# Dividing two more pairs of softmax rows ahead of their transposition, and starting the second batch's attention five steps earlier

## The chip, the cores and the metric

The kernel runs on one core of a Trainium2 chip. Its time is the device time of one execution in microseconds (us). Three executions of the kernel before took 2164.79 us (median), 2163.91 and 2167.59 us. Below, PE is the engine of the matrix multiplications (PEld its loading of the stationary operand), DVE the vector engine, ACT the scalar engine, POOL the general-purpose engine, and SP the engine that issues the DMA transfers.

## The reference: attention, a Fourier mix, and a two-layer network

```python
q_n, k_n = rmsnorm(q, g_q), rmsnorm(k, g_k)          # (8, 12, 448, 64)
scores = q_n @ k_n.T / 8
attn = exp(scores - max); attn = attn / (sum(attn) + 1e-9)
x = (attn @ v)  -> (8, 448, 768)                     # 8 batches, 12 heads side by side
X = fft(fft(x, axis=1), axis=2);  u = x + real(X)
un = (u - mean) / sqrt(var + 1e-6)
out = u + relu(un @ w_ch1) @ w_ch2                   # 768 -> 3072 -> 768
```

Everything is float32.

## The kernel before

**Batches and pairs.** A batch is one of 8 inputs of 448 tokens. Its 12 heads are handled as 6 pairs. In names such as `P0_4_2`, the numbers are batch, pair and row group: the 448 query rows of a pair are cut into 4 groups (c) of 112 rows.

**Attention of a pair** has three parts. `transpose_pair` loads q and k (`raw`), squares them on ACT, sums (`ss`), takes the power -1/2 on POOL, multiplies (`qkn`) and turns the two on PE (`qk`, copied by ACT to `QT` and `KD`). `softmax_pair` makes the scores `S` on PE, one bank per head, the row minimum `mn` on DVE, the exponential `P` with its row sum `sm` on ACT, and the reciprocal of `sm` on DVE. `value_pair` turns `P` (tiles `pt`, and a last piece `rem`), has ACT copy the turned tiles to `T` and `R`, and multiplies them with `v` into `av`; ACT copies that to `xT`.

**Two ways to divide the rows.** In batch 0 the rows stay undivided: DVE writes a diagonal matrix `dg` of the reciprocals, and the turning is a real matrix product of the piece with `dg`. In the other batches `P` is multiplied by the reciprocal first (head 0 on ACT and head 1 on DVE in batch 1) and the turning is PE's transposition against the identity `ident`.

**After attention.** `fold` (DVE: `eo`, `sd`, `tot`) adds and subtracts mirrored tokens and halves of the channels; `spectral` does the two Fourier steps as products (`y`, then `ab`), adds x back (`x`, `smdf`, `u`) and makes the centred rows `un`. `ffn_input` turns `un` into `unT`, and `ffn` runs the two layers, `h` (24 groups of 18 matmuls) and `o` (36 groups of 12), each product in three passes over high and low parts.

**What sets the order of work.** The attention and the spectral part are Python generators which give up control after each small step. The last part of the kernel first runs batch 0's generator alone: `for n, _ in enumerate(aux(0))`. It has 132 steps, n = 0 to 131: pair p = 5 of the attention takes n = 91 to 109, its values 110 to 120, a fold 121, the spectral part 122 to 131. At each step it may convert a part of the weights (`convert_some`; the conversions, `magw`, `dblw` and `w`, go through ACT, DVE and POOL in turn and are stored by DMA), and from n = `AHEAD_FROM` on it also takes one step of batch 1's generator, `second`. What `second` has not done by then is merged with batch 0's network by `merge`, in proportion to the costs that each step names. Within what is then written, a scheduler orders the instructions of each engine and places the waits. Each engine runs its own list strictly in order.

**Pair 0 of batch 1 has two callers.** In pair p = 5 of batch 0, `attention` calls `transpose_pair` for the next pair, which is pair 0 of batch 1. Batch 1's own generator begins with the same call. A test lets the second caller pass if the first has finished:

```python
        if b >= nb or (b, p) in ready:
            return
        load_pair(b, p)
        load_pair(*next_pair(b, p))
```

The first caller enters the pair into `ready` after its last step, when the loop that follows n = 109 resumes. `load_pair` loads nothing that still stands in `loaded`, but `norm_pair` takes the pair out of `loaded` when it begins.

**Banks.** A bank is one of eight accumulators of PE. `S` has two banks in rotation (also used by `y0_0_0`, `y0_1_0` and by `ab`), `PT` two (`pt`, `rem`, `y0_0_1`, `y0_1_1`), `ffn` two, `q` and `av` one each. PE cannot write a bank again before ACT or DVE has read it.

The functions that the diff touches, with the line numbers of the profile:

Of the kernel before, what the change touches and what calls it, by code (L numbers as in the profile page):

```python
# [43 lines left out]
DFT_STEP = 40  # L44
PLAIN_PAIRS = range(2 * NPAIR)
PLAIN_SCORES = range(2, 2 * NPAIR)
PACE = 3
LAG = 3
AHEAD_FROM = 112
AHEAD_STEPS = 1  # L50

MIN_HIGH = float(np.uint32(0x38000000).view(np.float32))
# [38 lines left out]
def spectral_block(ctx, tc, q, k, v, g_q, g_k, w1, w2, d1, d2, out, nb=B):  # L91
# [204 lines left out]
    def plain(b, p):  # L296


        return b * NPAIR + p in PLAIN_PAIRS

    def plain_s(b, p):
        return b * NPAIR + p in PLAIN_SCORES

# [56 lines left out]

    def softmax_pair(b, p, Pc):
        QT, KD, _ = ready[b, p]
        if b == 0:
            diags[b, p] = slot("h", f"dg{b}_{p}")[:C, : 8 * C].rearrange(
                "t (c h q) -> t c h q", c=NC, h=2
            )
        for c in range(NC):
            P = slot("P", f"P{b}_{p}_{c}")[:C, : 2 * S]
            Ph = [P[:, :S], P[:, S:]]
            mn = sb.tile([C, 2], F32, tag="mn", name=f"mn{b}_{p}_{c}", bufs=4)  # L370
            sm = sb.tile([C, 2], F32, tag="sm", name=f"sm{b}_{p}_{c}", bufs=4)
            cs = slice(c * C, (c + 1) * C)
            tag = "ffn" if b == 0 and c % 2 else "S"
            banks = [bank(tag, f"S{b}_{p}_{c}_{h}")[:C, :S] for h in range(2)]

            for h, s_ in enumerate(banks):
                hs = (lo, hi)[h]
                if plain_s(b, p):
                    nc.tensor.matmul(s_, QT[hs, cs], KD[hs], start=True, stop=True)  # L379
                    continue  # L380
                for step, K in enumerate((KD, KL)):
                    nc.tensor.matmul(  # L382
                        s_, QT[:, h, cs], K[:, h], start=step == 0, stop=step == 1
                    )
            for h, s_ in enumerate(banks):
                V.tensor_reduce(mn[:, h : h + 1], s_, axis=AX.X, op=ALU.min)
                A.activation(
                    Ph[h],
                    s_,
                    AF.Exp,  # L390
                    bias=mn[:, h : h + 1],
                    scale=-1.0,
                    accum_out=sm[:, h : h + 1],
                )
            A.activation(sm, sm, AF.Identity, bias=tiny[:C])
            V.reciprocal(sm, sm)
            if b == 0:
                V.tensor_tensor(
                    out=diags[b, p][:, c],
                    in0=ident[:C, None, :C].broadcast_to([C, 2, C]),  # L400
                    in1=sm[:, :, None].broadcast_to([C, 2, C]),
                    op=ALU.mult,
                )
                Pc.append(P)
                yield 760
                continue
            for h in range(2):
                if b < EARLY and h == 0:
                    A.activation(Ph[h], Ph[h], AF.Copy, scale=sm[:, h : h + 1])
                    continue  # L410
                V.tensor_scalar(
                    out=Ph[h], in0=Ph[h], scalar1=sm[:, h : h + 1], scalar2=None,
                    op0=ALU.mult,
                )
            Pc.append(P)
            yield 760

    def value_halves(b, p, Pc, xT, R):
# [3 lines left out]
        for j in range(3):  # L422
            T = []
            for h in range(2):
                pt = bank("PT", f"pt{b}_{p}_{h}_{j}")
                for c in range(NC):
                    piece = Pc[c][:, 512 * h + j * 128 : 512 * h + (j + 1) * 128]
                    if b == 0:
                        nc.tensor.matmul(  # L429
                            pt[:, c * C : (c + 1) * C], piece, diags[b, p][:, c, h],  # L430
                            start=True, stop=True,
                        )
                        continue
                    nc.tensor.transpose(
                        pt[:, c * C : (c + 1) * C], piece, ident[:C, :C]
                    )
                t = slot("PT", f"T{b}_{p}_{h}_{j}")[:, :S]
                copied = A.copy(t, pt[:, :S])
                T.append(t)
                yield 400  # L440
            for h, a in enumerate((lo, hi)):
                mm = nc.tensor.matmul(  # L442
                    av[a, :S], v_[:, j, h], T[h], start=j == 0, stop=False
                )
                if h == 0:
                    order(
                        mm, copied,
                        mybir.DependencyClass.Sync, mybir.DependencyReason.SCHED_ONLY,
                    )
            yield 800  # L450
# [8 lines left out]
    def value_pair(b, p, Pc, xT):  # L459
        vhl = ready[b, p][2]  # L460
        rem = bank("PT", f"rem{b}_{p}")
        for c in range(NC):
            if b == 0:
                for h, a in enumerate((lo, hi)):
                    nc.tensor.matmul(
                        rem[a, c * C : (c + 1) * C],
# [581 lines left out]
    for n, _ in enumerate(aux(0)):  # L1048
        if n == DFT_STEP:
            load_dft()  # L1050
        if n:
            convert_some(CONVERT_EARLY)
        if n >= AHEAD_FROM:
            for _ in range(AHEAD_STEPS):
                next(second, None)
    starting[0] = False
# [38 lines left out]
```

## Time and profile before

| | |
|---|---|
| median of three runs | 2164.79 us |
| the profiled execution | 2168.16 us, span 2166.3 us |
| mean granted clock of PE | 0.979 |
| PE busy | 2110.4 us (97% of the span) |
| DVE, ACT, POOL busy | 1523.5, 1122.6, 376.7 us |
| first matmul of the network of batch 0 (`h0_0`) | 188.87 us |

The profiled execution took 3.4 us more than the median of the runs. Rows of the timeline give the start and the length of each piece of work; in the chain of waits a piece is counted only as long as nothing else is ahead of it. A matmul of the program in plain float32 appears in the profile as two instructions, a transposition and a matmul of rounded halves as one. The granted clock says at what share of its full speed PE was allowed to run.

### The profile page before, as it was taken

To read this page: it belongs to the slowest core of one execution; us is meant where nothing else is said; L and a number is where in the kernel's file an instruction comes from. 1 tells how busy PE (TensorE), PEld (TensorE's weight loads), DVE (VectorE), ACT (ScalarE), POOL (GpSimd) and SP (SyncE) were. 2 spreads that over 40 slices of the span, in tenths; PEclk is the share of its full clock that TensorE was granted. 3 is DMA by queue.
4 is the path that set the end of the run, shared out by engine and by line. 5 is a ranking of instruction groups with operands and counts; after the bars stand their busy time and mean duration, and the time that the engine had idled before them with its cause. 6 is when DMAs were issued, how large, how long until landed. Compare 5 with 4: busy or idle time off the path is not lost.

```text
span 2166.3 us, 31520 instructions
## 1 busy us (share of the span) xinstructions
PE 2110.4 (97%) x11408; PEld 1845.1 (85%) x11408; DVE 1523.5 (70%) x2809; ACT 1122.6 (52%) x2462; POOL 376.7 (17%) x223
## 2 busy tenths in 40 slices
PE   7999999899999999999999999999999999999998
PEld 4555666789999999999999999999999999998998
DVE  6887778986885778758786678857787578743122
ACT  7877867465652566436652566526663466422100
POOL 4654555640110011001000001100110011000000
PEclk7988999999999999999999999999999999999999
DMA  6554867777556855667555765658555674459664
GB/s 198 183 161 143 258 237 214 250 261 221 160 166 185 252 164 167 193 189 220 173 168 176 236 185 173 192 171 234 179 176 177 206 213 147 152 172 280 196 214 151
DMA packets 294494, 422.12 MB, mean 195 GB/s; under 512 B 182994, under 2 KB 221315, under 8 KB 294340
## 3 DMA queue, kind: packets, MB, share of 16 engines
q1 hardware_dynamic: 293572, 419.43, 62.6%
q8 instruction: 91, 1.49, 0.3%
q10 hardware_dynamic: 768, 0.69, 0.1%
q14 instruction: 63, 0.52, 0.1%
HBM read 360.27 MB, written 65.28 MB: 196 GB/s over the span
## 4 chain that ended last, share of the span: by engine, by line
PE 86%; DVE 5%; ACT 2%; DMA 2%; issue 2%; POOL 1%; SPq 0%; POOLq 0%; DVEq 0%; ACTq 0%
PE h L981 30%; PE o L1002 30%; PE S L382 5%; PE av L502 4%; PE pt L490 4%; PE y L603 2%; DMA w<-w 2%; PE S L379 1%; PE qk L338 1%; PE pt L429 1%; PE av L442 1%; PE un L864 1%; PE x L635 1%; DVE magw L755 1%; PE oT L919 1%
## 5 line engine op out<-in xcount | busy, mean ns | idle before, releaser
L1002 PE MATMUL o<-hs,w 128*128 128x448 f32 x3420 | 776.7, 371 | 10.0 <-DMA w<-w 4.2
L981 PE MATMUL h<-unT,w 128*128 128x448 f32 x3402 | 767.6, 370 | 3.9 <-DMA w<-w 1.6
L1002 PEld LDWEIGHTS o<-hs,w 128*128 128x128 f32 x3420 | 634.2, 189 | 70.5 <-issue 12.2
L981 PEld LDWEIGHTS h<-unT,w 128*128 128x128 f32 x3402 | 628.8, 188 | 58.3 <-issue 4.8
L114 ACT ACTIVATE P<-S,mn 112x448 f32<-112x448 f32 x384 | 243.8, 637 | 206.0 <-DVE mn L114 200.2
L114 POOL TENSOR_TENSOR ss<-ss,nhalf 112x16 f32<-112x16 f32 x48 | 143.2, 2983 | 911.3 <-DVE ss L114 910.8
L114 DVE TENSOR_REDUCE mn<-S 112x1 f32<-112x448 f32 x384 | 234.6, 618 | 53.2 <-PE S L382 38.6
L114 ACT ACTIVATE hs<-h 128x448 fp32r<-128x448 f32 x192 | 104.3, 543 | 290.3 <-PE h L981 288.9
L114 DVE SCALAR_TENSOR_TENSOR hs<-h,hs 128x448 fp32r<-128x448 f32 x192 | 119.4, 622 | 149.2 <-ACT hs L114 147.8
L114 DVE TENSOR_TENSOR acc<-o,acc 128x448 f32<-128x448 f32 x240 | 148.5, 620 | 96.9 <-PE o L1002 95.7
L114 ACT CAST T<-pt 128x448 fp32r<-128x448 f32 x216 | 113.5, 532 | 91.9 <-PE pt L490 89.8
L114 DVE TENSOR_TENSOR T<-pt,T 128x448 fp32r<-128x448 f32 x216 | 132.6, 620 | 38.3 <-ACT T L114 36.9
L502 PE MATMUL av<-T,vhl 128*128 128x448 f32 x432 | 153.1, 384 | 0.0
L114 DVE TENSOR_SCALAR P<-P,sm 112x448 f32<-112x448 f32 x312 | 136.7, 475 | 5.0
L490 PE MATMUL pt<-ident,P 112*128 112x112 f32 x864 | 121.6, 259 | 0.0
L382 PE MATMUL S<-KD,QT 128*112 128x448 f32 x304 | 118.4, 391 | 3.0 <-ACT KD L114 3.0
L490 PEld LDWEIGHTS pt<-ident,P 112*128 112x128 f32 x864 | 102.8, 140 | 16.6
L382 PE MATMUL S<-rounded,QT 128*112 128x448 f32 x304 | 112.9, 373 | 0.0
L114 POOL TENSOR_TENSOR rstd<-st,nhalf 112x1 f32<-112x1 f32 (+2 forms) x32 | 18.8, 589 | 517.8 <-DVE st L114 517.8
L759 POOL TENSOR_TENSOR magw<-magw,dblw 128x512 uint32<-128x512 uint32 (+1 forms) x45 | 73.5, 1634 | 76.7 <-DVE magw L755 47.2
L502 PEld LDWEIGHTS av<-T,vhl 128*128 128x128 f32 x432 | 80.7, 188 | 6.7
L761 POOL TENSOR_TENSOR w<-magw,w 128x512 fp32r<-128x512 f32 (+1 forms) x45 | 74.9, 1668 | 36.7 <-ACT w L760 23.6
(140 smaller groups left out, 2650.0 us busy)
## 6 DMA issues: line engine op xcount, KB each, us to landing
w<-w SPq DMA_DIRECT2D x285, 512.0 KB, 4.0
w<-w SPq DMA_DIRECT2D x189, 768.0 KB, 5.2
dblw<-w SPq DMA_DIRECT2D x30, 512.0 KB, 4.2
dblw<-w SPq DMA_DIRECT2D x15, 768.0 KB, 6.3
raw<-q SPq DMA_DIRECT2D x96, 112.0 KB, 4.2
raw<-k SPq DMA_DIRECT2D x96, 112.0 KB, 2.8
v<-v SPq DMA_DIRECT2D x96, 96.0 KB, 2.6
u_dram<-u SPq DMA_DIRECT2D x24, 336.0 KB, 3.1
```

Of the source, the lines that this page charges most:

```text
L114: ins = emit(*args, **kwargs)
L338: nc.tensor.transpose(pt[:, c * C : (c + 1) * C], qk[:, i, c].rearrange("t h d -> t (h d)"), ident[:C, :C],)
L379: nc.tensor.matmul(s_, QT[hs, cs], KD[hs], start=True, stop=True)
L382: nc.tensor.matmul(s_, QT[:, h, cs], K[:, h], start=step == 0, stop=step == 1)
L429: nc.tensor.matmul(pt[:, c * C : (c + 1) * C], piece, diags[b, p][:, c, h], start=True, stop=True,)
L490: nc.tensor.transpose(pt[:, c * C : (c + 1) * C], Pc[c][:, 512 * h + j * 128 : 512 * h + (j + 1) * 128], ident[:C, :C],)
L502: nc.tensor.matmul(av[:, :S], lv, T[:, i], start=(j == 0 and i == 0), stop=False)
L603: nc.tensor.matmul(o, src[:, par, t0 : t0 + n], D1[:, ri, par, cols], start=i != 1, stop=i != 0,)
L759: behind(nc.gpsimd.tensor_tensor(out=bits, in0=bits, in1=low, op=ALU.add))
L761: behind(nc.gpsimd.tensor_tensor(out=part[1], in0=value, in1=part[0], op=ALU.subtract))
L981: pace(nc.tensor.matmul(o, w[:, a, c], unT[c][:, z], start=n == 0, stop=n == 17))
L1002: pace(nc.tensor.matmul(o, w[:, a, f], hs[4 * g + f][:, z], start=n == 0, stop=n == 11))
```

## The change

For pairs 4 and 5 of batch 0 the rows are divided before they are turned, as in the other batches, and no diagonal is made. Batch 1's generator takes its 20 single steps at n = 107 to 126 instead of n = 112 to 131.

```diff
+DIAG_PAIRS = range(4)
 PACE = 3
 LAG = 3
-AHEAD_FROM = 112
+AHEAD_FROM = 107
+AHEAD_UNTIL = 127
 AHEAD_STEPS = 1
...
+    def by_diagonal(b, p):
+        return b * NPAIR + p in DIAG_PAIRS
...
     def softmax_pair(b, p, Pc):
         QT, KD, _ = ready[b, p]
-        if b == 0:
+        if by_diagonal(b, p):
             diags[b, p] = slot("h", f"dg{b}_{p}")[:C, : 8 * C].rearrange(
...
             V.reciprocal(sm, sm)
-            if b == 0:
+            if by_diagonal(b, p):
                 V.tensor_tensor(
                     out=diags[b, p][:, c],
...
                     piece = Pc[c][:, 512 * h + j * 128 : 512 * h + (j + 1) * 128]
-                    if b == 0:
+                    if by_diagonal(b, p):
                         nc.tensor.matmul(
...
         rem = bank("PT", f"rem{b}_{p}")
         for c in range(NC):
-            if b == 0:
+            if by_diagonal(b, p):
                 for h, a in enumerate((lo, hi)):
...
-        if n >= AHEAD_FROM:
+        if AHEAD_FROM <= n < AHEAD_UNTIL:
             for _ in range(AHEAD_STEPS):
                 next(second, None)
```

At n = 107 pair 0 of batch 1 is not yet in `ready` and no longer in `loaded`. So batch 1's generator loads, normalises and turns this pair once more, in three of its 20 steps (n = 107, 108 and 109); the first group of its rows follows at n = 110, before at n = 112. At the end of the 20 steps batch 1 is three steps less far than before: a tile of values, the second group of pair 1's rows, and another tile of values are left to the merge.

The order shows this in three places. The first is ACT, where pair 3's values are copied while the rows of pair 4 are finished. Before:

```order
L114 ACTIVATE P0_4_3_987,sm0_4_3_989<-S0_4_3_0_990,mn0_4_3_988 112x448
L114 ACTIVATE sm0_4_2_954<-sm0_4_2_954,tiny_75 112x2
L114 ACTIVATE P0_4_3_987,sm0_4_3_989<-S0_4_3_1_991,mn0_4_3_988 112x448
L114 COPY xT0_136<-av0_2_714 128x448
L114 ACTIVATE sm0_4_3_989<-sm0_4_3_989,tiny_75 112x2
L114 COPY xT0_136<-xT0_136 128x1
L114 COPY T0_3_0_0_901<-pt0_3_0_0_896 128x448
L740 ACTIVATE magw2e27_918<-dblw2e27_919 128x512
L742 ACTIVATE dblw2e27_919<-dblw2e27_919 128x512
```

and in the changed kernel:

```order
L116 ACTIVATE P0_4_3_989,sm0_4_3_991<-S0_4_3_0_992,mn0_4_3_990 112x448
L116 ACTIVATE P0_4_0_869<-P0_4_0_869,sm0_4_0_871 112x448
L745 ACTIVATE magw1e0_1007<-dblw1e0_1008 128x768
L747 ACTIVATE dblw1e0_1008<-dblw1e0_1008 128x768
L116 ACTIVATE P0_4_1_903<-P0_4_1_903,sm0_4_1_905 112x448
L116 ACTIVATE sm0_4_2_955<-sm0_4_2_955,tiny_75 112x2
L116 ACTIVATE P0_4_3_989,sm0_4_3_991<-S0_4_3_1_993,mn0_4_3_990 112x448
L116 COPY xT0_136<-av0_2_714 128x448
L765 CAST w2e27_918<-magw2e27_919 128x512
L116 COPY T0_3_0_0_901<-pt0_3_0_0_896 128x448
```

Two divisions (`P0_4_0`, `P0_4_1`) and parts of two weight conversions now stand ahead of the copy `T0_3_0_0`; the first two instructions of the conversion `w2e27`, the last two rows shown of before, went still further ahead, in front of the copy `T0_2_1_2`.

The second place is PE at the end of batch 0's attention. Before:

```order
L379 MATMUL S1_0_0_0_1293<-KD1_0_1217,QT1_0_1187 112x448
L379 MATMUL S1_0_0_1_1294<-KD1_0_1217,QT1_0_1187 112x448
L442 MATMUL av0_5_1267<-T0_5_0_2_1343,v0_5_1051 64x448
L442 MATMUL av0_5_1267<-T0_5_1_2_1363,v0_5_1051 64x448
L452 MATMUL av0_5_1267<-R0_5_1265,v0_5_1051 64x448 x2
L379 MATMUL S1_0_1_0_1324<-KD1_0_1217,QT1_0_1187 112x448
L379 MATMUL S1_0_1_1_1325<-KD1_0_1217,QT1_0_1187 112x448
L379 MATMUL S1_0_2_0_1383<-KD1_0_1217,QT1_0_1187 112x448
L635 MATMUL x0_001_1515<-ident_68,xr0_0_1507 113x128 x3
L379 MATMUL S1_0_2_1_1384<-KD1_0_1217,QT1_0_1187 112x448
```

and now:

```order
L447 MATMUL av0_5_1315<-T0_5_0_2_1381,v0_5_1054 64x448
L447 MATMUL av0_5_1315<-T0_5_1_2_1416,v0_5_1054 64x448
L457 MATMUL av0_5_1315<-R0_5_1291,v0_5_1054 64x448 x2
L640 MATMUL x0_001_1569<-ident_68,xr0_0_1561 113x128 x3
L323 MATMUL qk1_0_0_1248<-ident_68,qkn1_0_1236 128x112 x4
L323 MATMUL qk1_0_1_1279<-ident_68,qkn1_0_1236 128x112 x4
L608 MATMUL y0_0_1_1467<-D1_82,eo0_0_1047 112x2x65
L608 MATMUL y0_1_1_1494<-D1_82,eo0_0_1047 112x2x65
L384 MATMUL S1_0_0_0_1303<-KD1_0_1284,QT1_0_1253 112x448
L384 MATMUL S1_0_0_1_1304<-KD1_0_1284,QT1_0_1253 112x448
```

The scores of batch 1's pair 0 moved behind the last values of batch 0, and behind a second turning `qk1_0` of the same pair (a first one stands further up in both kernels).

The third place is PE ahead of the network's first matmul. Before:

```order
L379 MATMUL S1_1_1_0_1625<-KD1_1_1503,QT1_1_1425 112x448
L635 MATMUL x0_100_1604<-ident_68,xr0_1_1602 112x128 x3
L635 MATMUL x0_101_1609<-ident_68,xr0_1_1602 112x128 x3
L379 MATMUL S1_1_1_1_1626<-KD1_1_1503,QT1_1_1425 112x448
L635 MATMUL x0_110_1639<-ident_68,xT0_136 112x128 x3
L635 MATMUL x0_111_1644<-ident_68,xT0_136 112x128 x3
L379 MATMUL S1_1_2_0_1766<-KD1_1_1503,QT1_1_1425 112x448
L864 MATMUL un0_1_1672<-ident_68,un0_1_1616 128x112
L864 MATMUL un0_1_1672<-ident_68,un0_2_1566 128x111
L864 MATMUL un0_3_1688<-ident_68,un0_1_1616 128x112
L864 MATMUL un0_3_1688<-ident_68,un0_2_1566 128x111
L379 MATMUL S1_1_2_1_1767<-KD1_1_1503,QT1_1_1425 112x448
```

and now (seven more transpositions `un0` follow the last row shown, and then `S1_1_2_0` and `S1_1_2_1` side by side):

```order
L384 MATMUL S1_1_1_0_1754<-KD1_1_1492,QT1_1_1429 112x448
L384 MATMUL S1_1_1_1_1755<-KD1_1_1492,QT1_1_1429 112x448
L640 MATMUL x0_100_1621<-ident_68,xr0_1_1619 112x128 x3
L640 MATMUL x0_101_1626<-ident_68,xr0_1_1619 112x128 x3
L640 MATMUL x0_110_1641<-ident_68,xT0_136 112x128 x3
L640 MATMUL x0_111_1646<-ident_68,xT0_136 112x128 x3
L869 MATMUL un0_0_1659<-ident_68,un0_0_1577 128x113
L869 MATMUL un0_0_1659<-ident_68,un0_1_1633 128x112
L869 MATMUL un0_0_1659<-ident_68,un0_2_1598 128x111
```

The scores of the two heads of a group (`S1_1_1_0` and `S1_1_1_1`, `S1_1_2_0` and `S1_1_2_1`) stood apart before and now follow each other; `S1_1_3_0` stays ahead of the network's first matmul, and `S1_1_3_1` went behind it. The tiles `pt1_0_0_0` and `pt1_0_1_0` of batch 1, before between the products `ab`, also went behind it.

## The prediction

> **What bounds the kernel now.** I read the shares of the chain of waits first, then the busy time of the engines stage by stage, then PE's granted clock in short windows, and last the timelines of the stages that the diff touches. The chain's shares by engine:
>
> ```profile
> PE 86%; DVE 5%; ACT 2%; DMA 2%; issue 2%; POOL 1%; SPq 0%; POOLq 0%; DVEq 0%; ACTq 0%
> ```
>
> The whole kernel is bound by PE. By stage (start:end and length, then busy us of PE, PEld, DVE, ACT and POOL with their instructions, granted clock, DMA share, GB/s) it looks otherwise at the beginning:
>
> ```profile
> 95.00:117.80 22.80, 21.68 (x115) 10.74 (x115) 19.24 (x35) 21.15 (x53) 12.48 (x8) 0.88 0.48 152
> 117.80:140.00 22.20, 22.20 (x158) 15.25 (x158) 18.20 (x28) 13.69 (x31) 7.58 (x5) 0.97 0.55 164
> 140.00:149.60 9.60, 6.31 (x21) 2.99 (x20) 8.62 (x16) 8.03 (x23) 6.91 (x4) 0.66 0.65 191
> 160.90:175.30 14.40, 9.33 (x44) 5.22 (x42) 11.13 (x27) 11.37 (x24) 5.58 (x6) 0.95 0.70 225
> 175.30:188.80 13.50, 13.44 (x31) 5.71 (x31) 7.50 (x24) 10.14 (x24) 1.64 (x3) 0.50 0.16 51
> 360.00:420.00 60.00, 51.07 (x259) 41.16 (x258) 54.16 (x69) 29.09 (x50) 34.94 (x20) 0.91 0.71 235
> 460.00:660.00 200.00, 200.00 (x1108) 182.71 (x1107) 157.81 (x299) 113.66 (x259) 22.41 (x10) 1.00 0.65 194
> ```
>
> From 460 us on PE has no gap and full clock: what comes later there stays late, and only work taken from PE makes it shorter. The change acts before. Pairs 4 and 5 of batch 0 lie in the first two rows: in the first PE and ACT are both nearly full (21.68 and 21.15 of 22.80 us), in the second PE alone (22.20 of 22.20). From 140 to 175 us PE has 8.4 us of gaps, since it waits for the folds and the spectral part. From 175.3 to 188.8 us it is full but at half clock. The clock in windows of 3.4 us (length, PE busy with its instructions, clock, DMA):
>
> ```profile
> 109.00:112.40 3.40, 2.30 (x11) 1.00 0.96 320
> 112.40:115.80 3.40, 3.40 (x8) 0.51 0.69 284
> 115.80:119.20 3.40, 3.40 (x13) 0.50 0.06 14
> ...
> 173.60:177.00 3.40, 1.64 (x2) 0.54 0.06 23
> 177.00:180.40 3.40, 3.40 (x10) 0.50 0.33 101
> 187.20:190.60 3.40, 3.40 (x9) 0.50 0.00 0
> ```
>
> A window with 1.1 us of gap was followed by two at half clock. A stall of PE here thus costs more than its length.
>
> **The change part by part.** First, what PE saves. Rows of the chain of waits (start, us, piece):
>
> ```profile
> 126.22 0.92 PE rem L465 x16
> 130.75 0.38 PE qk L318 x4
> 131.14 0.89 PE pt L429 x8
> 201.64 0.77 PE pt L434 x8
> 255.65 0.39 PE rem L471 x4
> ```
>
> A tile turned by the diagonal is eight instructions, 0.89 us; by transposition four, 0.39 us (0.77 for two tiles). Twelve tiles: 12 x 0.50 = 6.0 us. The last pieces: 2 x (0.92 - 0.39) = 1.1 us. The second turning of batch 1's pair 0 adds 2 x 0.38 = 0.8 us. So PE loses 6.3 us of work, of which nine tiles and one last piece (9 x 0.50 + 0.53 = 5.0 us) lie after 121.4 us, where PE is full.
>
> Second, what ACT and DVE take on. The groups of ACT's divisions and exponentials, DVE's divisions and diagonals (busy us, mean ns), then the ACT and PE rows around pair 3's first copy (start, us):
>
> ```profile
> L114 ACT ACTIVATE P<-P,sm 112x448 f32<-112x448 f32 x24 | 16.0, 668 | 8.5 <-DVE sm L114 8.5
> L114 ACT ACTIVATE P<-S,mn 112x448 f32<-112x448 f32 x384 | 243.8, 637 | 206.0 <-DVE mn L114 200.2
> L114 DVE TENSOR_SCALAR P<-P,sm 112x448 f32<-112x448 f32 x312 | 136.7, 475 | 5.0
> L114 DVE TENSOR_TENSOR dg<-ident,sm 112x224 f32<-112x224 f32 x24 | 21.0, 881 | 0.4
> ...
> 99.38 0.53 ACT L114 COPY T<-pt 128x448 f32<-128x448 f32 x1
> 99.81 0.68 ACT L740 ACTIVATE magw2e<-dblw2e 128x512 f32<-128x512 f32 x1
> 100.38 0.68 ACT L742 ACTIVATE dblw2e<-dblw2e 128x512 uint32<-128x512 uint32 x1
> 101.79 1.12 ACT L740 ACTIVATE magw1e<-dblw1e 128x768 f32<-128x768 f32 x1
> 103.58 1.07 ACT L114 ACTIVATE qkn<-raw 112x1024 f32<-112x1024 f32 x1
> 100.45 1.06 PE L429 MATMUL pt<-dg,P 112*128 112x112 f32 x8
> ```
>
> DVE exchanges eight diagonals (881 ns, 7.0 us) for eight divisions (475 ns, 3.8 us): no cost. ACT gets eight divisions; an ACT row starts about 0.1 us before the one ahead ends, so 0.57 us each, 4.6 us in all, into a stretch where it has 22.80 - 21.15 = 1.65 us idle. By the sum alone pair 4's first copy comes 3 us late. The order says more: ahead of `T0_3_0_0` now stand the w2e27 start (0.57 + 0.58), two divisions (1.1), the w1e0 start (103.58 - 101.79 = 1.8) and a cast (some 0.5, like the copy), together 4.6 us. The copy at 99.38 moves to about 104, PE's next tile (100.45) waits for its bank, and behind it in PE's list wait `av0_3` and pair 5's scores: PE stands about 3.5 us. Not all of it lasts, since that ACT work is then done. I put the delay at the start of pair 4's values at 2.5 us; bounds 1.7 (the 3.0 of the sum, less some gaps after 117.8 us, where ACT is busy 13.69 of 22.20) and 4.2 (one window at half clock on top, 1.7 us).
>
> After 121.4 us PE can regain at most 5.0 us, and 0.9 us more since `S1_0_0` moved behind the last values (row below, four instructions). But ACT must follow: two late divisions (1.1 us) and a conversion start (1.6 us, by the 1.8 above) now precede the copy `T0_5_0_2`. If these 2.7 us lie on the path, 3.2 of the 5.9 remain; 0.5, if they hold up the copies of both pairs in turn. I take 3.0. **End of batch 0's attention: 2.5 - 3.0 = -0.5 us**, bounds 1.7 - 5.9 = -4.2 and 4.2 - 0.5 = +3.7.
>
> Third, fold and spectral part. Rows of DVE in the last fold, then scores on PE and the last `un` on ACT:
>
> ```profile
> 141.59 1.14 DVE L114 TENSOR_TENSOR eo<-xT 128x449 f32<-128x449 f32 x2
> 142.65 0.62 DVE L114 TENSOR_REDUCE mn<-S 112x1 f32<-112x448 f32 x1
> 143.18 0.44 DVE L114 TENSOR_SCALAR P<-P,sm 112x448 f32<-112x448 f32 x1
> 144.62 0.62 DVE L114 TENSOR_REDUCE mn<-S 112x1 f32<-112x448 f32 x1
> 147.39 0.55 DVE L747 TENSOR_SCALAR magw1e<-magw1e 128x768 f32<-128x768 f32 x1
> 147.86 0.61 DVE L114 TENSOR_REDUCE mn<-S 112x1 f32<-112x448 f32 x1
> 148.47 1.07 DVE L114 SCALAR_TENSOR_TENSOR eo<-eo,eo 128x900 f32<-128x900 f32 x1
> ...
> 137.19 1.01 PE L379 MATMUL S<-KD,QT 64*112 64x448 f32 x4
> 158.45 1.00 PE L379 MATMUL S<-KD,QT 64*112 64x448 f32 x2
> 181.26 1.83 PE L379 MATMUL S<-KD,QT 64*112 64x448 f32 x2
> ```
>
> Batch 1's rows no longer stand inside the fold: minus 0.53 + 0.36 + 0.53 + 0.47 + 0.53 = 2.4 us (each row less the overlap of 0.08 to 0.09). Against that, `y0_0_0` and `y0_1_0` need the `S` banks, and now come after all four groups of that pair, each of which needs 2 x 0.53 us of DVE and 2 x 0.6 of ACT. I let the two cancel: **0**, bounds -2.4 and +1.5. ACT's copy `bs0_0` now stands behind the first group of pair 1 (two exponentials and a division, 1.8 us) where before it stood ahead: **+1.3**, 0 to 1.8.
>
> The last row group is the largest gain. The score of one head alone takes 1.00 us at full clock and 1.83 at half; two heads side by side take 1.01 together (they use different halves of the partitions). Between `x0_100` and `h0_0`, PE had five lone scores, 5 x 1.76 (1.83 less the overlap) = 8.8 us of the full 13.5 us before 188.8. Now it has one couple and one lone score, 3.5 us. **-5.3 us**, between -2 (if ACT's last `un` sets the end) and -7. Moved behind the first matmul at full clock: one lone score (0.9) and two tiles (0.8): **+1.7**.
>
> The other doubled work hides: the square (1.07 us) stands where pair 1's stood, POOL's power and products find POOL busy 7.58 of the 22.20 us, and four loads wait on SP for POOL's first `qkn`. Behind them in SP's list stand `v0_5`'s loads, which wait for pair 3's last values anyway; without that cover `av0_5` would be late by those four issues.
>
> Sum: -0.5 + 0 + 1.3 - 5.3 + 1.7 = **-2.8 us** on the profiled 2168.16 us. That execution stands 3.4 us over the median, so the forecast for the median is 2164.8 - 2.8 = **2162 us**. A measurement of this kernel can tell about 0.2%, 4.3 us, from no change, so this would mostly read as the same.
>
> **The rivals.**
>
> *The PE saving arrives whole.* ACT's delays vanish in its gaps, and the attention ends 4.2 us earlier instead of 0.5: -2.8 - 3.7 = -6.5, 2158 us. For it: PE is full from 117.8 to 140 us, where ACT has 8.5 us idle. Against it: the bank that waits for `T0_3_0_0`.
>
> *The clock gives the saving back (slower).* PE, with less to do and a stall at 100 us, falls to half clock in pairs 4 and 5's values, where before it had 0.97. The work from 121.4 to 140 us, 18.6 - 5.9 = 12.7 us at full clock, would take up to 25.4 at half, 6.8 us more than before instead of 3.0 less: -2.8 + 9.8 = +7.0 at the worst. With half of the work so (19.1 us) it is +0.7; I price the case at +5, 2170 us, a mean clock of 0.54. It decides against the change when the stretch's mean clock falls below about 0.7. For it: the window 109.00:112.40, and 177 to 190.6 us, where PE was full of transpositions and scores and stayed at 0.50. Against it: the same products `av` stand between the tiles as before.
>
> The Trainium skill, in "TensorE: Matmul & The Clock Gate", Part 4, says that PE in transpose mode does not count as busy for the gate that grants the clock. By that rule exchanging products for transpositions speaks for this rival; the full rows at 0.50 agree. Its Part 1 says that a busy window of some 3.4 us restores the clock, which by the same rows did not happen.
>
> *The network of batch 0 absorbs it.* Its order puts batch 1's spectral part 18 matmuls of the network later:
>
> ```profile
> 671.34 9.82 PE o L1002 x48
> ```
>
> 18 x 0.205 = 3.7 us. The stretch from 360 to 420 us, where PE has 8.9 us of gaps and DVE is 90% busy, then either moves with the rest or returns the gain: -2.8 + 3.7 = +0.9, 2166 us. Against it: the conversions, which fill DVE there, keep their places beside the network.
>
> **How the numbers follow.** Forecast 0.42, whole saving 0.24, clock 0.20, absorption 0.14. The stretches of the network reorder too, which gives each case some 4 us either way. Faster by over 0.2%: 0.85 of the whole saving and 0.35 of the forecast, 0.36 with a little of the absorption. Slower: 0.7 of the clock, 0.2 of the absorption, 0.08 of the forecast, 0.21, and 0.22 for what I have not seen. The same: 0.42. The range 2151 to 2173 reaches from the whole saving less 7 to the clock's price plus 3; the forecast's own is 2156 to 2168.
>
> **What would show it.** Right: the copy `T0_3_0_0` about 4 us later and PE idle ahead of `pt0_3_0_1`; pairs 4 and 5's tiles at four instructions; `y0_0_1` earlier than 149.6 us; two coupled scores before the network; `h0_0` between 181 and 187 us. Wrong: a clock under 0.7 between 118 and 140 us, `h0_0` at 189 us or later, or a first matmul that is early while the gaps from 360 to 420 us have grown by as much.

## The result: slower by 0.57%, and the profile after

| | before | changed |
|---|---|---|
| median, runs | 2165.99 us, 4 | 2179.29 us, 4 |
| all runs | 2163.91 to 2167.59 | 2174.58 to 2181.06 |
| ratio (95% interval) | | 1.0057 (1.0045 to 1.0070) |
| profiled execution, span | 2168.16, 2166.3 | 2174.58, 2172.4 |

The profiled execution of the changed kernel is the fastest of its four, 4.7 us below their median; that of the kernel before stood 3.4 us over the median shown ahead of the prediction. So the profiles differ by 6.4 us where the medians differ by 13.3. In later rounds the kernel before took 2160.1 to 2172.5 us, so small differences are read below from ratios with intervals, and a place in a profile only where several runs agree.

The chain of waits by engine, of the changed kernel:

```profile
PE 78%; DVE 1%; DMA 0%; ACT 0%; issue 0%; ACTq 0%
```

It adds up to 79%, not to 100, because here it can be followed back only to 439 us. It shows PE as the bound of what comes after that, and says nothing of the part in which the change acts. So the timelines have to carry the reading.

The stages of the prediction, in the changed kernel (start:end and length, then busy us of PE, PEld, DVE, ACT and POOL with their instructions, granted clock, DMA share, GB/s); between 140 and 200 us the stages are cut where they now lie:

```profile
95.00:117.80 22.80, 18.72 (x97) 10.10 (x96) 15.59 (x30) 19.37 (x49) 12.61 (x8) 0.93 0.55 165
117.80:140.00 22.20, 14.30 (x86) 7.72 (x84) 18.22 (x28) 18.32 (x38) 5.36 (x4) 0.92 0.45 142
140.00:151.50 11.50, 5.60 (x20) 2.49 (x20) 8.54 (x10) 4.32 (x9) 8.08 (x5) 0.55 0.58 148
151.50:171.40 19.90, 17.75 (x76) 12.66 (x76) 13.14 (x26) 12.32 (x31) 10.58 (x6) 0.67 0.27 80
360.00:420.00 60.00, 51.51 (x261) 40.42 (x259) 57.48 (x74) 36.46 (x65) 36.48 (x21) 0.95 0.75 246
420.00:460.00 40.00, 36.92 (x203) 33.65 (x204) 35.43 (x58) 22.69 (x41) 23.95 (x17) 0.95 0.66 232
```

From 117.8 to 140 us PE, which was full before, now stands 7.9 of 22.2 us. The work taken from it has become idle time. PE's timeline shows for whom it waits (start, us, instructions, and in brackets the idle time before them and what ended it):

```profile
102.75 1.39 PE L434 MATMUL pt<-dg,P 112*128 112x112 f32 x8 [3.37 <-ACT T L116]
122.23 0.60 PE L439 MATMUL pt<-ident,P 112*128 112x112 f32 x4 [3.23 <-ACT xT L116]
140.11 0.97 PE L447 MATMUL av<-T,v 128*64 128x448 f32 x4 [3.44 <-ACT T L116]
141.01 1.76 PE L457 MATMUL av<-R,v 64*64 64x448 f32 x4
151.49 1.21 PE L608 MATMUL y<-D,eo 128*112 128x130 f32 x4 [3.26 <-DVE eo L116]
152.63 1.83 PE L384 MATMUL S<-KD,QT 64*112 64x448 f32 x4
159.43 0.60 PE L323 MATMUL qk<-ident,qkn 112*128 112x112 f32 x4
166.18 1.21 PE L608 MATMUL y<-D,eo 128*113 128x130 f32 x4 [1.06 <-ACT P L116]
170.92 0.51 PE L608 MATMUL y<-D,tot 128*113 128x65 f32 x2
171.35 1.19 PE L384 MATMUL S<-KD,QT 64*112 64x448 f32 x2
173.94 0.79 PE L696 MATMUL ab<-Y,rounded 113*113 113x390 f32 x3
179.63 2.29 PE L696 MATMUL ab<-Y,rounded 112*112 112x390 f32 x6 [2.50 <-ACT bs L116]
190.72 1.49 PE L640 MATMUL x<-ident,xT 128*112 128x128 f32 x6
193.92 1.01 PE L384 MATMUL S<-KD,QT 64*112 64x448 f32 x4
198.87 0.59 PE L986 MATMUL h<-unT,w1e 128*128 128x448 f32 x1 [2.26 <-ACT unT L116]
```

The same pieces in the kernel before:

```profile
139.03 0.97 PE L452 MATMUL av<-R,v 64*64 64x448 f32 x4
160.57 0.32 PE L603 MATMUL y<-D,tot 128*113 128x65 f32 x2
177.09 1.54 PE L635 MATMUL x<-ident,xT 128*112 128x128 f32 x6
188.80 0.74 PE L981 MATMUL h<-unT,w1e 128*128 128x448 f32 x1
```

Where they end or start (us; the row puts `h0_0` of the kernel before at 188.80, the table ahead of the prediction at 188.87):

| | before | changed | difference |
|---|---|---|---|
| last `av` of batch 0 ends | 140.0 | 142.8 | +2.8 |
| last `y` ends | 160.9 | 171.4 | +10.5 |
| last `x` ends | 178.6 | 192.2 | +13.6 |
| `h0_0` starts | 188.8 | 198.9 | +10.1 |

In these two profiles nearly the whole loss lies ahead of `h0_0`. The largest step, 7.7 us, is between the end of the attention and that of `y`: at 152.63 us come the first scores of batch 1 (`S1_0_0`; before, they were done ahead of the last `av`), and `y0_0_0` starts only at 166.18, behind all four row groups of pair 1_0. The network then carries the loss on. The 48 `y` matmuls of batch 2 in the chain of waits, before and then changed:

```profile
681.16 5.11 PE y L603 x48
```

```profile
692.20 5.11 PE y L608 x48
```

That is 11.0 us; at the end of the span 6.1 are left. Of the 4.9 that come back, 2.1 are a wait of PE's for weights in the last 240 us, which is shorter in the kernel that arrives later (before, then changed: who waited for whom, total, times, longest):

```profile
PE o L1002 <- DMA w<-w: 3.6, 1, 3.6
```

```profile
PE o L1007 <- DMA w<-w: 1.5, 1, 1.5
```

### The profile page after: what moved, and what is told of

Its sections match the earlier page's. It is cut to its first block, busy times and chain, and to the rows that moved or that the text cites. A ratio compares the mean times of both kernels' runs of the same rounds, so it can differ in the third digit from the quotient of the medians.

```text
span 2172.4 us, 31408 instructions
## 1 busy us (share of the span) xinstructions
PE 2096.5 (97%) x11344; PEld 1837.2 (85%) x11344; DVE 1530.5 (70%) x2811; ACT 1127.6 (52%) x2473; POOL 376.9 (17%) x226
## 4 chain that ended last, share of the span: by engine, by line
PE 78%; DVE 1%; DMA 0%; ACT 0%; issue 0%; ACTq 0%
PE o L1007 29%; PE h L986 29%; PE S L387 5%; PE av L507 4%; PE pt L495 4%; PE y L608 1%; PE qk L343 1%; PE oT L924 1%; PE x L640 1%; PE un L869 1%; PE av L512 1%; PE rem L476 1%; PE ab L696 1%; DMA w<-w 0%; DVE magw L756 0%; DMA u_dram<-u 0%
## 5 line engine op out<-in xcount | busy, mean ns | idle before, releaser
L116 POOL TENSOR_TENSOR ss<-ss,nhalf 112x16 f32<-112x16 f32 x49 | 146.5, 2990 | 929.4 <-DVE ss L116 929.1
L116 DVE TENSOR_SCALAR P<-P,sm 112x448 f32<-112x448 f32 x320 | 143.5, 485 | 5.7
L116 DVE RECIPROCAL sm<-sm 112x2 f32<-112x2 f32 x192 | 31.1, 162 | 69.3 <-ACT sm L116 67.9
```

Of the source, the lines that this page charges most:

```text
L116: ins = emit(*args, **kwargs)
```

## The experiments

The theory after this reading: the moved steps cost, because they turn pair 1_0 a second time, so that its rows come late, and the two `S` banks hand that lateness on to `y0_0_0` and `y0_1_0`. Rivals: the division on ACT is the loss; or what batch 1 has not done by `h0_0` (three steps less) costs in the network. In the table "end" is the end of batch 0's last `av`, from one profiled execution each.

| run | division | steps n | median us | ratio (95%) | end | first `y` | `h0_0` |
|---|---|---|---|---|---|---|---|
| before | none | 112-131 | 2166 to 2167 | | 140.0 | 149.6 | 188.8 |
| changed | ACT+DVE | 107-126 | 2179.3 | 1.0057 (1.0045-1.0070) | 142.8 | 151.5 | 198.9 |
| 1 | ACT+DVE | 112-131 | 2173.0 | 1.0035 (1.0021-1.0050) | 146.6 | 159.1 | 199.2 |
| 2 | none | 107-126 | 2177.7 | 1.0054 (1.0039-1.0069) | 140.6 | 147.5 | 193.3 |
| 3 | ACT+DVE | 110-126 | 2172.4 | 1.0028 (1.0017-1.0039) | 145.6 | 155.1 | 192.9 |
| 4, `y` on ffn | ACT+DVE | 107-126 | 2182.1 | 1.0074 (1.0055-1.0093) | 144.8 | 153.6 | 198.2 |
| 5 | DVE only | 112-131 | 2173.9 | 1.0031 (1.0021-1.0041) | 137.3 | 149.8 | 192.5 |
| 6 | none | 110-126 | 2166.5 | 0.9993 (0.9982-1.0004) | 138.9 | 149.5 | 184.6 |
| 7 | none | 109-131 | 2173.8 | 1.0030 (1.0019-1.0041) | 140.3 | 148.5 | 197.7 |
| 8 | DVE only | 110-126 | 2168.1 | 1.0003 (0.9995-1.0012) | 139.8 | 149.7 | 187.4 |
| 9, `y`, `ab` on ffn | ACT+DVE | 107-126 | 2181.7 | 1.0067 (1.0053-1.0080) | 146.6 | 154.8 | 198.8 |
| 10, `y`, `ab` on ffn | none | 110-126 | 2167.5 | 1.0001 (0.9992-1.0010) | 139.6 | 150.2 | 184.5 |
| 11, `y`, `ab` on ffn | none | 112-131 | 2163.7 | 0.9984 (0.9975-0.9993) | 139.6 | 150.1 | 185.0 |
| 12, first turning read | ACT+DVE | 107-126 | 2181.6 | 1.0070 (1.0052-1.0087) | 145.1 | 155.0 | 199.2 |
| 13 | ACT+DVE | 107-124 | 2184.6 | 1.0077 (1.0065-1.0089) | 149.8 | 158.0 | 199.1 |
| 14 | ACT+DVE | 107-123 | 2184.3 | 1.0084 (1.0070-1.0097) | 142.8 | 151.5 | 190.1 |
| 15, `y`, `ab` on ffn | none | 110-124 | 2163.8 | 0.9987 (0.9977-0.9996) | 141.1 | 151.7 | 181.9 |

Where the steps start before n = 110, pair 1_0 is turned twice. Runs 1 to 10 bear the labels e1 to e10, runs 11 to 15 the labels e12 to e16.

### Runs 1 and 2: the two halves of the change

```diff
# run 1
-AHEAD_FROM = 107
-AHEAD_UNTIL = 127
+AHEAD_FROM = 112
+AHEAD_UNTIL = 132
# run 2
-DIAG_PAIRS = range(4)
+DIAG_PAIRS = range(6)
```

> Only the division of pairs 4 and 5 is moved; batch 1's single steps stay at n = 112 to 131. Theory (the loss comes from the moved steps: y0_0_0 and y0_1_0 wait for the S banks behind all row groups of pair 1_0): the attention of batch 0 ends within 140.6 +/- 2.5 us, y0_0_0 starts before 157 us, the spectral products y end by 163 us as before (160.9), h0_0 lies at 186 to 191 us, the time is 2161 to 2169 us. Rival 1 (the divisions on ACT and the stalls of PE behind them are the loss): h0_0 at 194 us or later, 2174 us or more. Rival 2 (the three steps less that batch 1 has done cost in the network): like the theory here, 2161 to 2169 us, since the steps are all done.

> Only the steps are moved (n = 107 to 126), all of batch 0 turns by the diagonal. Theory: y0_0_0 starts only after S1_0_3_1, at 163 us or later, y ends at 168 us or later, h0_0 at 196 to 201 us, the time is 2174 to 2181 us. Rival 1 (the division): as before, h0_0 at 187 to 191 us and 2162 to 2168 us. Rival 2 (the steps left to the network): h0_0 within 3 us of the 188.9 us of before, but the last product of the network late by 8 us or more.

Each half costs by itself: 0.35% and 0.54%. So the theory is right on the steps and wrong on the division, which was to be free. Run 1's time, 2173.0 us, lies between the two ranges that its expectation named. Both profiles are extreme: run 1's is the slowest of nine executions (2169 to 2181 us), run 2's the fastest of five (2173 to 2179), which may be why its `y0_0_0` (160.4 us) and `h0_0` (193.3) are earlier than expected. The halves do not add up (0.89% against 0.57%); one's delay may lie partly in the other's wait, which no run shows.

### Runs 3, 6 and 7: the repeated turning

```diff
# run 3
-AHEAD_FROM = 107
+AHEAD_FROM = 110
# run 6: run 3 without the division
-DIAG_PAIRS = range(4)
+DIAG_PAIRS = range(6)
# run 7: the kernel before, with the repetition alone
+DIAG_PAIRS = range(6)
+AHEAD_FROM = 109
+AHEAD_UNTIL = 132
```

> The whole change, but the single steps start at n = 110 instead of 107 (and end at 126 as well): the useful steps stand at the same n as in the changed kernel, and pair 1_0 is not loaded, normalised and turned a second time. y0_0_0 still stands behind all four row groups of pair 1_0 on the S banks. Theory with the repetition as what makes these rows late: the first rows of pair 1_0 come 6 us or more earlier than the 152.6 us of the changed kernel, y ends at 163 to 167 us instead of 171.4, h0_0 at 190 to 195 us, 2166 to 2173 us. If the order on the banks alone is the cause, whatever delays the rows: y0_0_0 at 164 us or later, h0_0 at 196 us or later, 2174 us or more. If rival 2 (three steps left over) is right: 2174 us or more with h0_0 below 193 us.

> Only the steps are moved, all of batch 0 turns by the diagonal, and the steps start at n = 110, so that pair 1_0 is not turned a second time (17 steps, n = 110 to 126). Theory (the repeated turning is what the moved steps cost: 2177.7 us with it): the rows S1_0 start before 140 us, h0_0 at 186 to 191 us, the time is 2163 to 2169 us. Rival (the three steps less, or the earlier rows themselves, cost): 2173 us or more.

> The kernel before, with the repeated turning of pair 1_0 and nothing else of the change: the steps start at n = 109, where the pair is not yet in `ready`; n = 109 to 111 go into the repetition, and the 20 steps of the kernel before follow at their own n = 112 to 131. Theory: the second qk1_0 comes behind the last values and the rows S1_0 start at 146 us or later instead of 137.2; h0_0 at 193 to 199 us, the time is 2171 to 2178 us. Rival (the repetition hides, the loss comes with the early start of the steps): 2163 to 2169 us.

Three pairs of kernels differ in the repetition, and it costs in each: changed against run 3, 6.9 us; run 2 against run 6, 11.3 us; run 7 against before, 7 us (by the ratios 0.29%, 0.61% and 0.30%). The early steps without it (run 6) cost nothing, although batch 1 is three steps less far, which rules out that rival at this size. PE's rows of run 3, then of run 7:

```profile
138.70 1.01 PE L384 MATMUL S<-KD,QT 64*112 64x448 f32 x4
152.22 1.01 PE L323 MATMUL qk<-ident,qkn 112*128 112x112 f32 x4 [1.65 <-POOL qkn L116]
192.86 0.74 PE L986 MATMUL h<-unT,w1e 128*128 128x448 f32 x1
```

```profile
144.87 1.01 PE L323 MATMUL qk<-ident,qkn 112*128 112x112 f32 x4 [2.18 <-POOL qkn L116]
154.13 2.51 PE L384 MATMUL S<-KD,QT 64*112 64x448 f32 x10
157.73 0.61 PE L323 MATMUL qk<-ident,qkn 112*128 112x112 f32 x4 [1.09 <-POOL qkn L116]
197.74 0.74 PE L986 MATMUL h<-unT,w1e 128*128 128x448 f32 x1
```

With the repetition the `qk` at 144.87 us is pair 1_0's second one, that pair's scores start at 154.1 instead of 137.2, and pair 1_1's `qk` follows at 157.7. Without it the first row is pair 1_0's scores and the `qk` at 152.22 is already pair 1_1's. Each turning needs POOL for its power and products, here in the changed kernel:

```profile
139.83 3.01 POOL L116 TENSOR_TENSOR ss<-ss,nhalf 112x16 f32<-112x16 f32 x1 [11.20 <-DVE ss L116]
144.04 2.43 POOL L116 TENSOR_TENSOR qkn<-raw,ss 112x512 f32<-112x512 f32 x2
155.35 2.90 POOL L116 TENSOR_TENSOR ss<-ss,nhalf 112x16 f32<-112x16 f32 x1 [7.27 <-DVE ss L116]
```

The first two are the repetition, between 139.8 and 146.5 us; pair 1_1's power comes at 155.35. In the kernel before it was this row:

```profile
140.77 2.90 POOL L114 TENSOR_TENSOR ss<-ss,nhalf 112x16 f32<-112x16 f32 x1
```

### Runs 4, 9, 10 and 11: the S banks

```diff
# runs 4, 9, 10, 11
-    Y_BANKS = (("S", "PT"), ("S", "PT"))
+    Y_BANKS = (("ffn", "PT"), ("S", "PT"))
# runs 9, 10, 11
-                o = bank("S", f"ab{b}_{t}_{i}")[:n, : NK]
+                o = bank("S" if b else "ffn", f"ab{b}_{t}_{i}")[:n, : NK]
```

Runs 4 and 9 are otherwise the changed kernel, run 10 is run 6, run 11 the kernel before.

> The whole change, but batch 0's y0_0_0 and y0_1_0 are written to the ffn banks, which nothing uses before the network, instead of the two S banks. Theory: y0_0_0 starts with y0_0_1 at about 151.5 us, the y products end at about 162 us instead of 171.4, the rows of pair 1_0 come later instead (behind y), h0_0 moves from 198.9 to 188 to 193 us, the time is 2164 to 2172 us. Rivals 1 and 2: y ends earlier, but h0_0 stays at 196 us or later, or the time stays at 2174 us or more.

> The whole change, with all of batch 0's spectral products off the S banks: y0_0_0, y0_1_0 and the four ab on the two ffn banks. With y alone moved, y ended at 164.2 us, but ab0_0_0 started at 175.9, behind the first rows of pair 1_1 on the S banks, and nothing was won. Theory (the S banks hand the lateness of pair 1_0's rows on to batch 0): ab starts by 168 us, h0_0 at 187 to 193 us, 2164 to 2173 us. Rival (ACT's and DVE's own lists, with DVE slowed beside POOL, hold the spectral part back, whatever banks it writes): ab at 172 us or later, or h0_0 at 196 us or later, 2176 us or more.

> All of batch 0 turned by the diagonal, the steps at n = 110 to 126 without repetition (2166.4 us), and y and ab of batch 0 on the ffn banks. If the S banks still hold the spectral part there: h0_0 at 178 to 184 us, 2156 to 2163 us, faster than both kernels. If, with the rows early, ACT and DVE bound it: 2163 to 2170 us, no change.

> The kernel before with y and ab of batch 0 on the ffn banks and nothing else. If the S banks hold the spectral part in the kernel before too: h0_0 at 181 to 187 us, 2157 to 2164 us. If not: 2164 to 2170 us.

The banks are not the cause. In run 4 `y` ends at 164.2 us as wanted, and nothing is won. In run 9 `ab` too starts at once (PE's rows, and between them one of ACT):

```profile
166.15 0.77 PE L696 MATMUL ab<-Y,rounded 113*113 113x390 f32 x3
180.07 1.29 PE L696 MATMUL ab<-Y,rounded 112*112 112x390 f32 x3
198.83 0.74 PE L986 MATMUL h<-unT,w1e 128*128 128x448 f32 x1 [1.38 <-ACT unT L116]
```

```profile
178.21 0.47 ACT L116 COPY bs<-ab 113x390 f32<-113x390 f32 x1
```

but ACT copies `bs` at 178.2, behind the exponentials of pairs 1_0 and 1_1 in its own list, and `h0_0` is as late as ever. By these rows the late rows stand ahead of the spectral part on more than one engine at once, so that freeing the banks alone leaves the lists. Run 11 has no late rows, and there the banks give 0.16%, with run 15 the fastest version measured; the interval lies clear of no change, the difference under the 0.2% that the prediction gave as the least a measurement can tell. In run 10 they give nothing.

### Runs 5 and 8: who divides

```diff
# runs 5 and 8: both heads on DVE in batch 0
-                if b < EARLY and h == 0:
+                if 0 < b < EARLY and h == 0:
```

Run 5 has run 1's steps, run 8 those of run 3.

> As the division alone (steps at n = 112 to 131), but in pairs 4 and 5 of batch 0 DVE divides both heads, so that ACT gets none of the eight divisions. Theory (the divisions on ACT, which is full from 95 to 106 us and from 118 to 129 us, hold up the copies T and with them PE): PE no longer stands 3.4 us ahead of the tile after T0_3_0_0, the attention of batch 0 ends at 137 to 141.5 us instead of 146.6, the time is 2160 to 2168 us instead of 2173. Rival a (the transpositions let PE's clock fall, whoever divides): the attention ends at 143 us or later with a mean clock below 0.85 between 117.8 and 140 us, the time is 2170 us or more. Rival b (DVE takes 1.0 us for such a division while POOL works, as it did in the runs so far, and becomes the bound itself): DVE over 90% busy between 100 and 130 us, PE waits for DVE's P, 2170 us or more.

> The whole change without its two suspected costs: both heads' divisions of pairs 4 and 5 on DVE, and the steps at n = 110 to 126, without the repeated turning. Theory (divisions on ACT and repetition are the whole loss): 2158 to 2167 us, h0_0 at 182 to 189 us. If DVE is the bound with the divisions, or the three steps left over cost: 2170 us or more.

That the divisions on ACT hold up the attention is borne out. In the eight profiles where ACT divides, the attention ends 2.8 to 9.8 us later than before; in the two where DVE does it alone, 2.7 and 0.2 us earlier; in the six without the division it lies within 1.1 us. Part of the spread from 2.8 to 9.8 is PE's clock (last section). But run 5's time does not follow. In windows of run 5:

```profile
117.80:140.00 22.20, 18.25 (x95) 8.28 (x93) 20.70 (x33) 14.41 (x33) 6.45 (x4) 0.86 0.54 162
140.00:150.00 10.00, 2.12 (x11) 1.30 (x10) 10.00 (x15) 6.11 (x15) 10.00 (x5) 0.72 0.40 139
```

DVE is 93% busy in the first, as rival b said, and in the second DVE and POOL are full together while PE stands: its longest wait there, 7.88 us up to 148.98, is for POOL's products `qkn`, whose turning stands ahead of the first `y` in its list. From the end of the attention to the first `y` it takes 12.5 us in runs 1 and 5, 9.6 in the kernel before: the fold and POOL's conversions and products meet there. This uses up the 2.7 us by which run 5's attention ends earlier. The 3.7 us by which its `h0_0` is late come between the last `y` and the last `x` (22.4 us, before 17.7), and 4.0 us more behind `h0_0`; what causes these two is not traced. With the steps of run 8 the stretch ahead of the first `y` is 9.9 us again, and the whole change is back at no difference (1.0003; 2168.1 us, 1 us above what the theory allowed). That the fold and POOL hold each other up is read from these rows; no run takes POOL's work away alone.

### Runs 12 to 15: how the repetition costs

```diff
# run 12: the second turning is done, but its result is not used
-            ready[b, p] = T[0], T[1], vhl
+            ready.setdefault((b, p), (T[0], T[1], vhl))
...
-        ready[b, p] = QT, KD, vhl
+        ready.setdefault((b, p), (QT, KD, vhl))
# run 13
-AHEAD_UNTIL = 127
+AHEAD_UNTIL = 125
# run 14
+AHEAD_UNTIL = 124
# run 15: run 10 with
+AHEAD_UNTIL = 125
```

> The whole change, with the repeated turning of pair 1_0 still done in full (loads, square, sums, power, products on POOL, transpositions, copies), but the rows of the pair read QT and KD of the first turning, since the second does not replace the entry in `ready`. It tells the wait for the second turning from its work. Theory (the rows wait for the second turning, which comes out of POOL at about 148 us): S1_0_0 starts before the last values again, at about 140 us or earlier instead of 152.6, and the time falls to that of the whole change without repetition, 2168 to 2175 us. Rival (the repeated work itself, on POOL beside DVE's fold and ahead of pair 1_1's turning, is the loss): S1_0_0 early as well, but h0_0 at 196 us or later and 2176 us or more.

> The whole change, but the single steps end at n = 124: the last two, with which the rows of pair 1_1 begin, are left to the merge, so that S1_1_0 no longer stands ahead of batch 0's ab in PE's list. The repeated turning and all of its work stay. If its place is what costs (pair 1_1's turning comes one turning later, and S1_1_0 and its exponentials hold up ab and bs): ab starts at once behind y, h0_0 at 187 to 194 us instead of 198.9, the time is 2166 to 2174 us. If the work costs (POOL beside DVE's fold): h0_0 at 196 us or later, 2177 us or more.

> As the run before it, but the steps end at n = 123, so that pair 1_1's second transposition goes to the merge too, and none of that pair's rows come before the network of batch 0. By the place: h0_0 at 184 to 192 us; the time is 2164 to 2174 us, unless the work left to the network costs more there (then h0_0 early and 2174 us or more). By the work: h0_0 at 195 us or later, 2176 us or more.

> No division, no repetition: steps at n = 110 to 124, y and ab of batch 0 on the ffn banks. With the steps up to 126 this took 2167.5 us; the kernel before with the same banks took 2163.7. If fewer of batch 1's rows ahead of the network help by themselves: h0_0 at 178 to 183 us, 2156 to 2163 us. If they only pay where the turning is late: 2163 to 2169 us.

Run 12 fells the obvious reading that the rows wait for the second turning. Its PE rows:

```profile
139.09 1.01 PE L384 MATMUL S<-KD,QT 64*112 64x448 f32 x4
169.32 1.01 PE L323 MATMUL qk<-ident,qkn 112*128 112x112 f32 x4
172.33 2.05 PE L384 MATMUL S<-KD,QT 64*112 64x448 f32 x4 [0.72 <-ACT KD L116]
174.94 3.86 PE L696 MATMUL ab<-Y,rounded 113*113 113x390 f32 x12
199.16 0.74 PE L986 MATMUL h<-unT,w1e 128*128 128x448 f32 x1 [1.40 <-ACT unT L116]
```

The scores of pair 1_0 are early, `y` ends at 164.3 like run 3's, and still all is lost again: pair 1_1's turning comes one turning later (169.3 against 152.2 us in run 3), its first scores stand ahead of `ab` in PE's list, and `ab` starts at 174.9.

Runs 13 and 14 take these rows away from there. From the end of the attention to `h0_0` it is then 49.4 and 47.3 us instead of 56.1 (48.8 before), so the place of these rows does cost. It is not `ab` alone that gains: of run 14's 8.8 us, 4.5 lie ahead of the last `y`, 1.3 between it and the last `x`, and 3.1 behind. Run 13's attention ends 7.0 us later than the changed kernel's, so that its `h0_0` (199.1) and its time fall where the expectation put the case that the work costs. In neither does the time get better. Run 14's `h0_0` and a window of its network:

```profile
190.07 0.74 PE L986 MATMUL h<-unT,w1e 128*128 128x448 f32 x1 [0.23 <-ACT unT L116]
```

```profile
420.00:460.00 40.00, 30.18 (x165) 27.65 (x164) 37.40 (x47) 16.52 (x29) 23.99 (x14) 0.87 0.59 210
```

`h0_0` is 1.3 us late, batch 2's `y` 17.7 us (they end at 704.0, in the kernel before at 686.3). In this window PE is busy 30.18 and DVE 37.40 of 40 us (before: 38.17 and 35.88). So the rival that run 6 had ruled out may return for more steps: with three steps missing, run 6 loses nothing after `h0_0`; with five or six, runs 13, 14 and 15 lose 8.2, 16.4 and 5.4 us between `h0_0` and batch 2's `y`. But runs 1 and 5, which leave no step over, lose 5.9 and 4.0 us there too, and runs 9 and 12, which leave three, 5.5 and 6.3, so only run 14's loss stands clear. Run 15 gains 6.9 us ahead of `h0_0` and gives 5.4 of them back; its time falls where the expectation put the case that fewer rows do not help by themselves.

What is settled: the repetition costs some 7 us or more, and neither the banks nor the wait for its result are the way. In the rows shown it takes one turning's place on POOL and PE, and batch 1 is late by that, ahead of `h0_0` in the changed kernel and behind it, as far as one profile shows, in run 14. Open: how much of it is the place in the lists and how much POOL's work beside DVE.

## Why the prediction was wrong, step by step

Predicted 2162 us (2151 to 2173); measured 2179.3, 6 us above the upper end.

Two steps failed, and the runs price both. In medians the way back from the changed kernel is 6.9 us by leaving out the repetition (run 3) and 6.0 more by leaving out the division (run 6), which brings it to no difference. Leaving out the division first gives 1.6 us (run 2), and the repetition then 11.3, so the split depends on the order.

- **The step that failed: "The other doubled work hides".** I gave the second turning 0.8 us of PE and nothing else, on the ground that POOL was busy 7.58 of 22.20 us. That room was read in the wrong stretch, 117.8 to 140 us. The work came at 139.8 to 146.5 us, and from 140 to 149.6 us POOL was busy 6.91 of 9.60 us before, with pair 1_1's own power and products among it. These now came behind the repetition. Price by the runs: 7 to 11 us. That pair 1_0 is turned twice stood in the text; that a piece off the critical path delays the next of its kind did not.
- **Fold, "0, bounds -2.4 and +1.5".** From the end of the attention to the end of `y`: 20.9 us before, 28.7 changed, 18.6 in run 3. Without the repetition the term is -2.3, inside its bounds; with it, +7.8. The term was sound for rows that come as early as they did before.
- **The second step that failed: end of the attention, "-0.5 us", bounds -4.2 and +3.7.** Measured +2.8, and in runs 4, 9 and 13, whose PE and ACT lists are the same up to there, +4.8, +6.6 and +9.8. The first half was right in kind: PE stood 3.37 us (forecast 3.5), though the copy `T0_3_0_0` came 2.7 us later (102.1 instead of 99.4) and not 4.6. The 3.0 us to be regained were not: two more copies came late on ACT, and PE stood 3.23 us at 122.2 and 3.44 at 140.1. Ahead of the first stand a division and parts of two conversions. Ahead of the second stand a square and the starts of two conversions, and no division; run 2 (early steps, no such divisions) shows 2.40 us at the same place and run 1 (divisions, no early steps) 0.96, so this stall came with the early steps. The price of DVE's part was wrong too: 475 ns each was taken from a mean over the whole kernel; here it was 441 to 2107 ns.
- **`bs0_0` behind pair 1_1, "+1.3", bounds 0 to 1.8.** From the last `y` to the last `x`: 17.7 us before, 20.8 changed, 23.3 in run 3. +3.1 and +5.6, outside: not only `bs` but pair 1_1's scores on PE stand ahead.
- **Coupled scores, "-5.3", between -2 and -7.** From the last `x` to `h0_0`: 10.2 us before, 6.7 changed, 5.4 and 6.0 in runs 3 and 6. -3.5 to -4.8: right in kind and within its bounds; the couple is the row at 193.92 us. Cut where the prediction counted, from `x0_100` on, the term is -6.9 (16.4 us before, 9.5 changed), still inside, and the term of `bs0_0` grows to +6.4.
- **Moved behind `h0_0`, "+1.7".** By batch 2's `y` the loss has grown by 0.9 us (from 10.1 to 11.0), with whatever else the network changed in it.
- **Signs named ahead.** Right: the stall, tiles of four instructions, the couple; in part the copy (2.7 us later, not 4). Wrong: the first `y` at 151.5, not before 149.6; `h0_0` at 198.9 where 189 or later was named as refuting.
- **Rivals.** The saving did not arrive whole. The clock did not fall where the rival put it (0.92 from 117.8 to 140 us, its limit was 0.7); it fell ahead of it, after the stall at 100 us, for a time that differed from profile to profile (below). The network absorbed nothing of +10.1 us up to batch 2's `y`. The range's upper end, 2173, came from the clock's price; no rival had the repetition in it.

## What to carry to other kernels

When a change moves the start of a generator, ask what its first steps do at the new moment: here they did not see a result that was not yet entered as ready, and made it again. Work that "hides" on a half-idle engine still takes a place in an ordered sequence, and the idle time must be read at the moment when it comes; price it by what the next of its kind does to its consumers, and test it by leaving it out alone. An engine's operation must be priced where it will stand: an exchange of PE's work for ACT's or DVE's is paid at the copies that PE waits for, and a gain ahead of a join may be given back behind it.

## What the runs showed of the hardware that was not expected

**DVE waits out a conversion on POOL.** DVE's divisions in the changed kernel (least, median, most ns), one of them, and POOL's row at that time:

```profile
L116 DVE TENSOR_SCALAR P<-P,sm x8: 441/828/2107, 96.7 to 124.0; 112x448 f32<-112x448 f32 x8
```

```profile
101.47 2.11 DVE L116 TENSOR_SCALAR P<-P,sm 112x448 f32<-112x448 f32 x1
```

```profile
101.49 1.83 POOL L764 TENSOR_TENSOR magw1e<-magw1e,dblw1e 128x768 uint32<-128x768 uint32 x1 [3.91 <-ACT P L116]
```

The division ends 0.26 us behind POOL's instruction, 2.11 us for 0.44 us of work. Two more, at 120.41 and 124.03 us, end 0.25 us behind conversions on POOL. The Trainium skill, "SBUF — State Buffer", section "SBUF: two separate sides", says that some DVE operations share a port pair with GpSimd (here POOL) under an exclusive lock, held for a whole instruction. These rows agree. The fold's first rows (`eo`, 3.33 us for two at 143.63 us, 1.14 in the kernel before) lie beside a conversion and the products on POOL (142.80 to 146.47 us). Beside the power it is less regular: in the kernel before, the same `eo` (141.59 to 142.73 us) and a division of 0.44 us at 143.18 lie wholly inside the power of 140.77 to 143.67 and show no wait, while in run 5 a division inside the power of 141.43 to 144.71 took 1.44 us.

**The same stall is followed by a shorter or a longer time at half clock.** The 8 us behind the end of the stall at 100 us, in the changed kernel and in run 13, whose PE and ACT lists are the same up to the end of the attention:

```profile
102.75:110.75 8.00, 8.00 (x40) 4.72 (x40) 4.83 (x9) 5.29 (x11) 6.59 (x4) 0.79 0.47 164
```

```profile
104.94:112.94 8.00, 8.00 (x26) 4.93 (x28) 3.10 (x6) 4.85 (x10) 6.60 (x4) 0.50 0.48 164
```

PE is full in both, with 40 instructions at 0.79 and 26 at 0.50, and the attention ends 7 us apart. Run 13 came to the stall 2.2 us later; 3.0 us more are lost from there to 114.67 and 119.84 us, where both start the same scores, and 1.8 behind them. Read in windows of 0.1 us, the half clock lasted 3.5 us in the changed kernel and runs 3 and 14, 6.9 to 7.0 us in runs 4, 9 and 12, and 10.3 us in runs 1 and 13: steps of about 3.4 us. The stall was 3.4 us in all eight, and the later PE was done with it (102.75 to 104.94 us), the longer the half clock lasted; what sets the length is not shown. In the five of them with the same lists, the attention ends 2.8 us later than before with 3.5 us of half clock (changed and run 14), 4.8 and 6.6 with about 7 (runs 4 and 9), and 9.8 with 10.3 (run 13). I had priced it at one window of 3.4 us, 1.7 us lost at most. By the same sum, an estimate, three windows lose 5.1 us.
